# Batch 1's q and k transposed by TensorE instead of the DMA crossbar, in a fused attention and FFN kernel

## Chip, cores, metric

One core of one Trainium2 chip. The metric is the device time of one execution in microseconds (us). The kernel before took 269.71 us, the median of three runs (269.7 to 271.35); its profiled run took 265.9 us, with a span of 264.1 us in the trace.

## The reference

Block-sparse attention over 4 batches, 8 heads, 768 positions of 64 elements, then a multiplicative feed-forward layer:

```python
scores = (1/sqrt(64)) * q @ k.T           # per batch and head, 768 x 768
scores = where(mask, scores, -1e9)        # window, global and sampled 32-blocks
attn   = softmax(scores)
x      = (attn @ v), heads concatenated   # 3072 x 512
h      = (x @ w1) * (x @ w2)              # 512 -> 1024
out    = (h @ w3) @ w_out                 # the kernel folds w3 @ w_out into wf
```

## The kernel before

A planner in the program lists the work as tasks with guessed costs, orders them by a list schedule, and emits the instructions in that order. On the chip each engine then works through its own list in that order. In one unit of attention (a head pair and 256 queries) ScalarE takes the exponentials of scores (`e<-s`), VectorE multiplies by the mask and, after the value matmuls (`o<-v,e`), normalizes into `xn`.

q and k arrive with positions on the partitions and must be turned so that the 64 elements lie there. Batch 0 is turned by TensorE (`if b == 0`), the other batches by a relayout copy on VectorE and a transposing DMA from the SP queue:

```python
mid = ("qs", b, pr, x)                               # pool "qs" has 3 buffers
m = add(f"re {b}{pr}{x}", {DVE: 0.37}, ... nc.vector.tensor_copy(T(*mid), ...), deps=[LD[src]], ...)
t = add(f"xb {b}{pr}{x}", {SP: 1.25}, ... nc.sync.dma_start(out=T(*dst)..., in_=T(*mid)..., transpose=True),
        deps=[m], writes=[dst], reads=[mid], kind="xbar", prio=1)
```

The normalized rows `xn` go through the same crossbar, from the same SP queue, into `x`, which the w1 and w2 matmuls read. The planner's guess for a crossbar transfer hardly depends on what else the DMA engines do:

```python
elif t.kind == "xbar":
    xbar = max(xbar, t.end + 0.6) + t.bytes / 250e3
    t.seen = max(xbar + 0.4, t.end + (4.0 if lane > t.end else 1.2))
```

There is one accumulator buffer `o` in PSUM (where the matmuls write), two for the scores, and eight for the exponentials.

The softmax here doesn't subtract the row's maximum and nothing guards it: scores larger than these inputs give would overflow.

## Time and profile before

| | before, profiled run |
|---|---|
| span | 264.1 us |
| TensorE busy | 243.5 us (92%) |
| ScalarE, VectorE busy | 189.5, 174.8 us |
| mean granted clock (share of TensorE's full clock) | 0.948 |
| first w1 matmul | 71.04 us |

Loads move 14.7 MB as written, in 0.98 us for 192 KB, and fill the DMA engines up to about 85 us.

The prediction shows the slices, the waits and the hole at 45 to 52 us. A share of busy time says little here: the last 190 us are TensorE's without a gap, so only the first third has anything to win.

### The profile page before, as it was taken

The page shows a single profiled execution, that of the slowest core. Times are in us where ns is not written, and L with a number is a line of the kernel's source. Part 1 is how long each engine was busy: PE and PEld are TensorE (multiplying, and loading weights), DVE is VectorE, ACT ScalarE, POOL GpSimd, SP SyncE. Part 2 cuts the span into 40 slices and gives each one's busy share as a digit, 9 for nine tenths or more (in the row PEclk, how much of TensorE's full clock was granted, in tenths as well). Part 3 has the DMA queues.
Part 4 walks back from the last instruction along what each step waited for, and adds up shares of the span by engine and source line. Part 5 has one row for each costly group of instructions (what it writes and reads, how often), then busy time and mean ns, then how long its engine had stood idle before and what let it go on. Part 6 is the DMA issues. An engine that isn't in the chain of part 4 may idle for free.

```text
span 264.1 us, 6276 instructions
## 1 busy us (share of the span) xinstructions
PE 243.5 (92%) x2516; PEld 129.5 (49%) x2556; DVE 174.8 (66%) x381; ACT 189.5 (72%) x237; POOL 45.9 (17%) x75
## 2 busy tenths in 40 slices
PE   6888998099899999999999999999999999999993
PEld 2446655055454555554555455455554555444441
DVE  5585761268978888888888877857777787322420
ACT  3677766149988898998988988898987885324331
POOL 8943564512223112411000000000000000000000
PEclk9655799869999999999999999999999999999999
DMA  5999999999999819999229702033020231112013
GB/s 71 164 204 210 206 200 195 204 187 145 183 165 105 125 30 126 265 180 181 41 65 198 121 4 40 2 99 102 4 40 2 60 102 43 39 57 103 2 40 119
DMA packets 52193, 29.25 MB, mean 111 GB/s; under 512 B 33732, under 2 KB 47044, under 8 KB 52164
## 3 DMA queue, kind: packets, MB, share of 16 engines
q0 software_dynamic: 16416, 14.68, 37.1%
q1 hardware_dynamic: 35748, 14.16, 26.7%
q8 instruction: 20, 0.33, 0.5%
q14 instruction: 9, 0.07, 0.1%
HBM read 29.36 MB, written 6.29 MB: 135 GB/s over the span
## 4 chain that ended last, share of the span: by engine, by line
PE 84%; DMA 7%; ACT 3%; issue 3%; POOL 1%; DVE 0%; POOLq 0%; DVEq 0%; ACTq 0%
PE f L577 32%; PE f L596 16%; PE s L484 15%; PE o L506 15%; DMA qkt<-qs 5%; PE f L558 3%; ACT e L491 2%; DMA qn<-in_q_dram 2%; PE f L435 2%; PE f L412 2%; PE f L546 1%; ACT wf L271 0%; POOL qn L305 0%; DVE qs L444 0%; POOL kn L305 0%
## 5 line engine op out<-in xcount | busy, mean ns | idle before, releaser
L491 ACT ACTIVATE e<-s 128x1024 bf16<-128x1024 f32 x144 | 139.9, 1026 | 23.9 <-PE s L484 22.7
L493 DVE TENSOR_TENSOR e<-e,mask 128x1024 bf16<-128x1024 bf16 x144 | 94.0, 684 | 6.3 <-ACT e L491 6.1
L577 PE MATMUL f<-x,w 128*128 128x512 bf16 x361 | 93.2, 379 | 2.4 <-issue 1.3
L506 PEld LDWEIGHTS <-e 128*128 128x128 bf16 x1152 | 49.2, 100 | 36.7 <-DVE v L458 7.6
L506 PE MATMUL o<-v,e 128*128 128x65 bf16 x1152 | 57.8, 198 | 6.9 <-DVE v L458 6.8
L588 DVE TENSOR_TENSOR h<-f,a 128x512 bf16<-128x512 f32 x48 | 33.0, 687 | 28.7 <-PE f L577 26.9
L484 PE MATMUL s<-qkt 64*128 64x256 bf16 x576 | 47.8, 283 | 2.1 <-ACT e L491 1.6
L596 PE MATMUL f<-wf,h 128*128 128x512 bf16 x180 | 46.2, 379 | 0.8 <-issue 0.3
L577 PEld LDWEIGHTS <-w 128*128 128x128 bf16 x384 | 31.3, 97 | 29.4 <-issue 4.6
L585 ACT CAST a<-f 128x512 bf16<-128x512 f32 x48 | 28.2, 588 | 23.4 <-PE f L577 23.3
L484 PEld LDWEIGHTS <-qkt 64*128 64x128 bf16 x576 | 22.6, 95 | 30.9 <-issue 26.8
L596 PEld LDWEIGHTS <-h 128*128 128x128 bf16 x192 | 16.0, 98 | 14.7 <-issue 1.3
L514 DVE RECIPROCAL rec<-o 128x4 f32<-128x4 f32 x48 | 8.7, 180 | 20.0 <-PE o L506 19.8
L271 ACT COPY ob<-f 128x512 f32<-128x512 f32 x21 | 12.3, 587 | 13.1 <-PE f L596 11.9
L516 DVE TENSOR_TENSOR xn<-o,rec 128x256 bf16<-128x256 f32 x48 | 20.4, 424 | 1.7
L305 POOL DMA_DIRECT2D qn<-in_q_dram x16 | 11.6, 725 | 33.2 <-DVE qs L444 22.9
L305 POOL DMA_DIRECT2D vn<-in_v_dram x16 | 11.6, 723 | 27.9 <-DVE xn L516 19.0
L558 PE MATMUL f<-wo,w3t 128*128 128x512 bf16 x59 | 15.4, 392 | 0.8 <-ACT w3t L271 0.2
L305 POOL DMA_DIRECT2D kn<-in_k_dram x16 | 11.5, 721 | 20.8 <-DVE qs L444 13.9
L444 DVE COPY qs<-kn 128x768 bf16<-128x768 bf16 x12 | 4.3, 360 | 8.9 <-DMA qkt<-qs 8.9
L558 PEld LDWEIGHTS <-w3t 128*128 128x128 bf16 x64 | 5.8, 100 | 7.2 <-issue 1.5
L271 ACT CAST wf<-f 128x512 bf16<-128x512 f32 x8 | 4.7, 587 | 4.3 <-PE f L558 4.2
(50 smaller groups left out, 81.5 us busy)
## 6 DMA issues: line engine op xcount, KB each, us to landing
out_dram<-ob SPq DMA_DIRECT2D x24, 256.0 KB, 2.1
qn<-in_q_dram POOLq DMA_DIRECT2D x16, 192.0 KB, 6.3
kn<-in_k_dram POOLq DMA_DIRECT2D x16, 192.0 KB, 6.1
vn<-in_v_dram POOLq DMA_DIRECT2D x16, 192.0 KB, 7.3
w3n<-in_moe_w_dram POOLq DMA_DIRECT2D x8, 256.0 KB, 12.5
w<-in_moe_w_dram POOLq DMA_DIRECT2D x8, 256.0 KB, 10.0
wo<-in_moe_w_out_dram POOLq DMA_DIRECT2D x2, 512.0 KB, 11.0
qkt<-qs SPq DMA_TRANSPOSE x24, 6.4
```

The costliest lines, as they stand in the source:

```text
L271: (nc.scalar.copy if t.eng == ACT else nc.vector.tensor_copy)(out, in_)
L305: t = add(name, {POOL: 0.73}, lambda t: nc.gpsimd.dma_start(out=out_of(), in_=src), deps=deps, writes=writes, kind="load", prio=seq[0])
L484: nc.tensor.matmul(s[:, h, k2 * QT:(k2 + 1) * QT], lhsT=z[64 * h:64 * h + 64, 1, kc * 128:(kc + 1) * 128], rhs=z[64 * h:64 * h + 64, 0, t3 ...
L491: te = add(f"E {ek}", {ACT: 0.97}, lambda t, sk=sk, ek=ek: nc.scalar.activation(T(*ek), T(*sk), AF.Exp, scale=1.0 / 8.0), deps=[ts], reads ...
L493: tm = add(f"K {ek}", {DVE: 0.70}, lambda t, ek=ek, t3=t3, kp=kp: nc.vector.tensor_tensor(T(*ek), T(*ek), mask[:, t3, kp:kp + 1, :].to_bro ...
L506: nc.tensor.matmul(o[:, qt, h, :], lhsT=e[:, h, lo:lo + 128], rhs=w[:, h, kc, :], start=kc == 0 and qt == 0 and h == 0, stop=kc == C - 1, ...
L516: tx = add(f"xn {rk}", {DVE: 0.42}, lambda t, rk=rk, ok=ok, xk=xk, pr=pr: nc.vector.tensor_tensor(T(*xk)[:, :, 128 * pr:128 * pr + 128].re ...
L558: nc.tensor.matmul(T(*key), lhsT=T("w3t", i)[:, j, :], rhs=wo_sb[:, j, :], start=j == 0, stop=j == NF - 1)
L577: nc.tensor.matmul(T(*key), lhsT=w[:, c, f * 128:(f + 1) * 128], rhs=T(*xk)[:, c, :], start=c == 0, stop=c == 3)
L585: ta = add(f"a {i}{f}", {ACT: 0.58}, lambda t, ak=ak, key=ends["w1"][0]: nc.scalar.copy(T(*ak), T(*key)), deps=[ends["w1"][1]], reads=[end ...
L588: nc.vector.tensor_tensor(T(*hk)[:, f, :], T(*key), T(*ak), op=ALU.mult),
L596: nc.tensor.matmul(T(*key), lhsT=T(*hk)[:, f, n * 128:(n + 1) * 128], rhs=wf_sb[:, f, :], start=f == 0, stop=f == NF - 1)
```

## The change

Its intent: keep batch 1 off the crossbar while the loads run, and bring w1 and w2 in earlier so that the feed-forward matmuls can fill TensorE. The core of the diff:

```diff
-         "p10 p11 p12 p13 10 20 11 21 12 22 13 23 "        # loads: pairs of batch 1, then w1/w2
+         "10 20 11 21 12 22 13 23 p10 p11 p12 p13 "
-WARM = 8                                                  # warming matmuls at the start
+PRM = dict(..., trb=8, units="tttt", warm=0.0)            # one; "spare" ones never run at warm=0
-                xbar = max(xbar, t.end + 0.6) + t.bytes / 250e3
-                t.seen = max(xbar + 0.4, t.end + (4.0 if lane > t.end else 1.2))
+                at = t.start
+                for a, z, row in lanes:                   # every load in flight delays it
+                    if a < at + 1.25 <= z:
+                        at += 4.5 * row / 4096            # row: 4096 weights, 1536 q, k, v
+                t.end = at + 1.25
+                t.seen = t.end + 1.6 + 0.6 * (at - t.start)
-        "qs": ([128, C, 2, D], BF16, 3, None),
+        "qs": ([128, C, 2, D], BF16, 4, None),
-            if b == 0:
+            if (b, pr) in by_pe:                           # b * NP + pr < 8: batches 0 and 1
-                        prio=1)
+                        prio=1 if b == 0 else 4)
 ... (priority of the copies of batch 1; code for other unit orders, not used)
```

More of the change, by code (lines that the diff above doesn't have):

```diff
@@ L20 @@
 LOADS = ("a01 v00 a02 v01 a03 v02 v03 o0 o1 30 31 32 33 34 35 36 37 "
-         "p10 p11 p12 p13 10 20 11 21 12 22 13 23 "
+         "10 20 11 21 12 22 13 23 p10 p11 p12 p13 "
          "p20 p21 p22 p23 p30 p31 p32 p33")
-WARM = 8
 PRM = dict(bias=0.4, bmask0=1.0, bmask=1.0, btc=0.5, near=0.12, soon=0.06, kprio=2.0, eprio=0.5, aprio=1.0,
-           hprio=1.0, vprio=1.5, w3prio=10.0, ebufs=8, both=0.25, fo="31", pcopy=4.0)
+           hprio=1.0, vprio=1.5, w3prio=10.0, ebufs=8, both=0.25, fo="31", pcopy=4.0, trb=8, units="tttt",
+           warm=0.0)
 LONG = ("load", "xbar", "store")
@@ L51, in __init__ @@
         self.slots = defaultdict(list)
-        self.pool_of = {}
+        self.spare = None
     def add(self, name, costs, go, deps=(), writes=(), reads=(), kind="", prio=0, mode="N", flight=0.0, bias=None):
@@ L103, in run @@
         lane = 0.0
-        xbar = 0.0
+        lanes = []
         mode = "N"
@@ L132, in run @@
                     picks.append((p[0], eng, p[1]))
+            if self.spare and free["PE"] < PRM["warm"]:
+                pe = min([p[0] for p in picks if p[1] == "PE"], default=1e9)
+                rest = min([p[0] for p in picks if p[1] != "PE"], default=1e9)
+                if pe > free["PE"] + 0.2 and rest > free["PE"]:
+                    w = self.spare(mode)
+                    w.start, w.end, w.eng = free["PE"], free["PE"] + w.costs["PE"], "PE"
+                    free["PE"] = w.end
+                    self.log.append(w)
+                    continue
+            elif self.spare:
+                self.spare = None
+                self.left[("f", "warm")] = 0
+                self.freed[("f", "warm")] = free["PE"] + SEEN["PE"]
             picks.sort(key=lambda p: (p[0], p[1]))
@@ L141, in run @@
             if t.kind == "load":
-                lane = max(lane, t.end + 1.75) + t.bytes / 375e3
+                from_ = max(lane, t.end + 1.75)
+                lane = from_ + t.bytes / 375e3
+                lanes.append((from_, lane, t.row))
                 t.seen = lane + 0.2
@@ L146, in run @@
             elif t.kind == "xbar":
-                xbar = max(xbar, t.end + 0.6) + t.bytes / 250e3
-                t.seen = max(xbar + 0.4, t.end + (4.0 if lane > t.end else 1.2))
+                at = t.start
[3 more added lines that the diff above has]
+                t.end = at + 1.25
+                free[eng] = t.end
+                t.seen = t.end + 1.6 + 0.6 * (at - t.start)
                 for key in set(t.writes) | set(t.reads):
@@ L307, in load @@
         t.bytes = nbytes
+        t.row = 1536 if name.startswith("ld") else 4096
         return t
@@ L361, with spare @@
     t_zero = add("zero", {DVE: 0.2}, lambda t: nc.vector.memset(zero, 0.0), prio=-1)
-    for i in range(WARM):
-        add(f"warm {i}", {PE: 0.427}, lambda t: nc.tensor.matmul(
-            T("f", "warm"), lhsT=zero[:, :128], rhs=zero, start=True, stop=True),
-            deps=[t_zero], writes=[("f", "warm")], prio=-1)
+    add("warm", {PE: 0.43}, lambda t: nc.tensor.matmul(
+        T("f", "warm"), lhsT=zero[:, :128], rhs=zero, start=True, stop=True),
+        deps=[t_zero], writes=[("f", "warm")], prio=-1)
+    plan.users[("f", "warm")] += 1
+    def spare(mode):
+        rows = 64 if mode == "S" else 128
+        return Task("spare", {PE: 0.11}, (), (), (), lambda t: nc.tensor.matmul(
+            T("f", "warm")[:, :256], lhsT=zero[:rows, :128], rhs=zero[:rows, :256], start=True, stop=True),
+            "spare", 0, mode, 0.0)
+    plan.spare = spare
     def dve(name, cost, deps, go, **kw):
@@ L421 @@
     QK, V1 = {}, {}
+    by_pe = [(b, pr) for b in range(B) for pr in range(NP) if b * NP + pr < PRM["trb"]]
     def prepare(b, pr):
@@ L437, in prepare @@
                 m = add(f"tr {b}{pr}{x}", {PE: 0.35 + SWITCH}, tr, deps=[LD[src], t_ident], writes=[key], reads=[src],
-                        prio=1)
+                        prio=1 if b == 0 else 4)
                 done.append(add(f"tc {b}{pr}{x}", both(0.81, 0.56), lambda t, key=key, dst=dst, x=x: copy_on(
                     t, T(*dst)[:, x, :], T(*key, shape=[128, S], dt=BF16)), deps=[m], writes=[dst],
-                    reads=[key], prio=0, bias={ACT: -0.3 * x if pr == 0 else PRM["btc"]}))
+                    reads=[key], prio=0 if b == 0 else 3, bias={ACT: -0.3 * x if b + pr == 0 else PRM["btc"]}))
             else:
@@ L469 @@
     for b in range(B):
-        units += [(b, t, pr) for t in range(NT) for pr in range(NP)]
+        how = PRM["units"][b]
+        if how == "t":
+            units += [(b, t, pr) for t in range(NT) for pr in range(NP)]
+        elif how == "Q":
+            units += [(b, t, 2 * Q + i) for Q in range(2) for t in range(NT) for i in range(2)]
+        else:
+            units += [(b, t, pr) for pr in range(NP) for t in range(NT)]
     Xdone = defaultdict(list)
```

## The prediction

> **What bounds the kernel now.** I read the page's slices first, then the waits, then the timelines of the engines around the hole that the slices show, then the crossbar's own queue. Section 2 of the page, each column 6.6 us:
>
> ```profile
> PE   6888998099899999999999999999999999999993
> DVE  5585761268978888888888877857777787322420
> ACT  3677766149988898998988988898987885324331
> PEclk9655799869999999999999999999999999999999
> DMA  5999999999999819999229702033020231112013
> ```
>
> From the eleventh slice on TensorE is at 9 everywhere: the last 190 us are bound by matmul work, 98 to 99% busy (118.02 us busy of the 120 from 100 to 220 us, by a table of windows), with 3.9 us of ending after the last matmul. So time can only be won or lost in the first 75 us. There stands one hole, the eighth slice, where TensorE, VectorE and nearly ScalarE are all at 0 or 1 while the DMA engines stay at 9; right after it the granted clock is down too. The waits say who was held:
>
> ```profile
> DVE qs L444 <- DMA qkt<-qs: 9.3, 2, 8.9
> PE o L506 <- DVE v L458: 6.8, 1, 6.8
> ```
>
> and the timelines of VectorE, TensorE and the SP queue show the chain:
>
> ```profile
> 42.27 0.07 DVE L458 MEMSET v<- 128x12 bf16 x1
> 51.44 0.36 DVE L444 COPY qs<-kn 128x768 bf16<-128x768 bf16 x1 [8.88 <-DMA qkt<-qs]
> 51.71 0.17 DVE L514 RECIPROCAL rec<-o 128x4 f32<-128x4 f32 x1
> ...
> 44.72 0.84 PE L546 MATMUL f<-ident,w3n 128*128 128x128 bf16 x12
> 52.41 1.50 PE L506 MATMUL o<-v,e 128*128 128x65 bf16 x24 [6.84 <-DVE v L458]
> ...
> 71.04 1.02 PE L577 MATMUL f<-x,w 128*128 128x512 bf16 x3 [0.54 <-issue]
> ...
> 37.78 17.65 SPq L447 DMA_TRANSPOSE qkt<-qs  x4
> ```
>
> The fourth relayout copy of batch 1 needs one of three qs buffers; the first is free only when its crossbar transpose lands, 13.54 us after issue in the chain of the end. VectorE runs in order, so the reciprocal and normalization behind that copy wait too. They hold the only o accumulator, so the next value matmuls cannot start, and TensorE stands still from 45.5 to 52.4 us. The crossbar is slow because the loads fill the DMA engines: four transposes took 17.65 us to issue there, against 1.21 us for a single one at 135.62 us, when the queue is idle.
>
> The clock is the second loss. Windows of half a microsecond show it granted 0.50 from 50.3 to 57.15 us; TensorE was busy 4.52 of the 4.74 us from 52.41 on, so half of that, about 2.2 us, is lost.
>
> **What the Trainium skill says.** "TensorE: Matmul & The Clock Gate", Part 1, puts the clock down to half after an idle window of about 3.4 us and up again after a busy one. The trace agrees: it fell once 4.8 us into the hole and rose 4.7 us after work resumed. It is less simple at the start: the 0.50 from 9.37 to 29.85 us lay over a TensorE about 95% busy. Part 4 of the same page gives 275 to 390 ns for one transpose on TensorE and asks for a copy from PSUM after it. The trace has 314 ns median for one, but twelve in flight took 0.53 us at a granted 1.00 (0.46 us to the next matmul) and 0.71 to 0.77 us at 0.50, so the figure is a latency and the pitch is what counts. "DMA: Bandwidth & Descriptors", Queues, rings and completion order, says that each DMA engine takes turns between its queues by packet; that fits a crossbar transfer that stretches while the load queue is full. "TensorEngine Tiling (Array Packing)", Key Properties, says that a change of tiling mode drains TensorE; the 0.46 us above contains such a drain if there is one, so I add none.
>
> **The change, part by part.**
>
> 1. Batch 1's q and k by TensorE. The eight relayout copies on VectorE (8 x 0.36 = 2.9 us) and eight crossbar transposes go. The hole (6.84 us) goes with its cause, and the cold 6.8 us after it: 2.2 us. Added are 96 transposes: 8 groups x 0.46 = 3.7 us on TensorE, all on the bound, and eight copies from PSUM, four on ScalarE (0.80 each) and four on VectorE (0.56). If nothing else came into it: -6.84 - 2.2 + 3.7 = -5.3 us.
>
> 2. Loads behind w1 and w2. Load pitch in the trace is 0.98 us for a q, k or v and, by the bytes, 1.31 us for a weight block; 8 weight blocks move ahead of 9 smaller loads. From the issues I place the end of the w3 loads at about 34 us; then in the new order come 8 x 1.31 + 0.98 (one v of batch 0) = 11.5 us, so q of batch 1, pair 0 lands near 46.6 us, and each pair 2.9 us after the last. In the built order its transposes stand 9.5 us of work after the value matmuls of 44 us, at about 52 us; the second pair lands near 50 and is asked for near 56. I expect no wait for these loads.
>
> 3. What TensorE has to fill the time. This is the part that the diff hides, and the order shows. In the kernel before, the first w1/w2 matmul stands after 132 score matmuls (33 exponentials) and 240 value matmuls; in the changed one after 172 (43 exponentials) and 312. The wo/w3 products, which filled the gaps between 53 and 68 us before, are pulled forward into the place of the hole. After them there is a run of attention alone: 13 exponentials with nothing else for TensorE but two groups of transposes. There ScalarE sets the pace: two exponentials take 1.94 us, while their scores (8 in 0.54 us) and values (16 in 0.59) take 1.13.
>
>  Counting ScalarE: through 47.1 us both orders are the same, 19 exponentials. The score pair that follows the two value groups comes at about 48 us (V at 45.0, since six more wo/w3 products at 0.216 precede it; 0.9 + 0.43 + 0.55 + 0.9 + 0.27 of work after). From there to the first w1 matmul ScalarE does 22 exponentials x 0.97 = 21.3, four copies of 0.80 = 3.2 and one of 0.6: 25.1 us, to about 73.3 us. VectorE has about as much: from 45.9 us 26 mask products x 0.66, 11 normalizations x 0.56 and about 6 us of copies, 29 us, to the first product h near 75. TensorE's own work in that stretch is 240 V x 0.037 + 96 S x 0.0675 + 3.7 + 18 x 0.216 + 16 x 0.07 = 24 us, so it would be idle for some 4 to 5 us, in small pieces.
>
>  So the changed kernel starts w1 at 73.3 to 74.3 us rather than 71.04, but has done 40 score and 72 value matmuls more: 2.7 + 2.7 = 5.4 us of bound work. The lead is 5.4 - 2.3 to 3.3 = 2.1 to 3.1 us. After that both are bound by the same matmuls.
>
> 4. One warming matmul for eight. At the start the eight ran at 634 ns each and the clock stood at full for one window, 5.96 to 9.37 us by the clock records. With one, that window will likely be cold: twelve k transposes go from 0.53 to 0.85 us, and the first scores are late by as much. Cost about 0.3 us. The spare matmuls in the diff never run, as their limit is 0.
>
> 5. A fourth qs buffer and fewer crossbar transposes (24 to 16 for q and k) keep batches 2 and 3 from the same jam; there is no wait of that kind in TensorE's time after 75 us, so I give it nothing.
>
> Sum: -2.6 (middle of the lead) + 0.3 = -2.3 us by the trace. The trace's run took 265.9 us, though, and the timed ones 269.7; I do not know where those 3.8 us lie. If part of them is a longer hole or cold stretch, the change wins it back as well. I add a fifth of it, 0.8 us: 269.7 - 3.1 = 266.6.
>
> **The rivals.** (a) The hole closes and nothing takes its place: TensorE stays bound from 45 us on, which gives the -5.3 + 0.3 of step 1, 264.7 us; with the missing 3.8 us in the hole, 261. For it: two s and eight e buffers give slack, and x may come early. Against it: the engine's order is fixed, and the first w1 matmul stands behind the 43rd score group whatever x does. (b) ScalarE and VectorE become the bound for 15 us, as in step 3: 267.4, or 266.6 with the allowance. (c) The thin stretch of attention cools the clock: TensorE near 57% busy there, while it cooled at 9.37 us after a window 53% busy, but not at 46.9 after one of 60%. Two cold windows would cost 2 to 3 us: about 269. (d) A transpose stands in TensorE's order before its load has landed, and everything behind waits: each microsecond of lateness costs one. The 4 to 6 us of slack in step 2 speak against it. (e) The x transposes, now issued while weights stream, land late and hold the first w1 matmul: at 9.3 us to landing, seen before, the second pair, issued near 58, lands by 68, before 73.
>
> **Range and chances.** b is my main case with half the weight, a has a quarter, c, d and e share the rest. That gives 262.8 to 270.0 us for 8 in 10. The 2% line lies at 264.3 us; only a, or b with most of the unexplained 3.8 us, crosses it: 0.28. Slower than 275.1 would need c and d together: 0.03.
>
> **What would show it.** Step 1: no wait of VectorE for qkt<-qs, no zero in TensorE's slices, a clock at 9 from 30 us on, and about 3.7 us in 96 more transposes. Step 2: no wait of TensorE's transposes on qn or kn beyond the first pairs of batch 0. Step 3: first w1 matmul at 73 to 74 us, ScalarE over 90% busy from 55 to 72 us, TensorE idle 4 to 5 us from 46 to 74 in pieces under a microsecond. Step 4: a cold start up to about 30 us. I am wrong if w1 starts before 70 us (then a), if the clock falls between 60 and 75 us (c), or if TensorE has a wait over 2 us for a load or for x (d, e).

## More of the kernel before

From section 6 of the page, with the size in KB and the median microseconds from issue to landing as the last columns (a transpose has no size there):

```profile
w<-in_moe_w_dram POOLq DMA_DIRECT2D x8, 256.0 KB, 10.0
qkt<-qs SPq DMA_TRANSPOSE x24, 6.4
x<-xn SPq DMA_TRANSPOSE x24, 3.8
```

## The result, and the profile after

The changed kernel took 262.54 us, the median of 4 runs (261.72 to 264.28), against 270.53 us (269.7 to 273.14) for the kernel before: faster, ratio 0.970, 95% interval 0.961 to 0.978. Ratios here are the mean time of one kernel's fast runs over that of the other's in the same rounds, so not quite the ratio of the medians quoted. That it would be faster by over 2% was given a chance of 0.28, and the time lies just under the range (262.8 to 270.0).

The slices of the changed kernel, each 6.5 us:

```profile
PE   2988999999899999999999999999999999999993
DVE  5485942998988898889888877788787743412420
ACT  3577964999999688998898998888998844233321
PEclk9999999999999999999999999999999999999999
DMA  5999999999569699998427330212302033022013
```

The zero in TensorE's row is gone. The one soft place after the start is the eleventh slice (65 to 71 us), where ScalarE is at 9 and TensorE at 8. The clock's row needs care: the first clock record of this trace comes at 26.8 us, and the row shows 9 before it only because there is none. Twelve transposes took 0.85 us there, as they did at a granted 0.50, and 0.53 from 50 us on: the start was cold, as step 4 foretold.

The timeline of TensorE in the changed kernel (start, duration, line and operation, count):

```profile
44.03 0.89 PE L541 MATMUL o<-v,e 128*128 128x65 bf16 x24
...
46.50 0.61 PE L519 MATMUL s<-qkt 64*128 64x256 bf16 x8
...
50.09 0.53 PE L464 MATMUL f<-ident,qn 128*64 128x128 bf16 x12
...
71.95 0.39 PE L612 MATMUL f<-x,w 128*128 128x512 bf16 x1
```

Batch 1's first transposes run at 50.09 us and wait for nothing. The first w1 matmul comes at 71.95 us, 0.9 us later than in the profile of before, with 40 score and 72 value matmuls more behind it. By windows (busy time and count of TensorE, its weight loads, VectorE, ScalarE, GpSimd; then clock, DMA share, GB/s), the changed kernel:

```profile
44.00:60.00 16.00, 15.46 (x290) 10.87 (x293) 13.75 (x31) 14.70 (x18) 5.71 (x8) 1.00 1.44 166
60.00:75.00 15.00, 13.02 (x213) 8.08 (x213) 13.64 (x33) 14.60 (x17) 3.13 (x5) 1.00 0.74 107
75.00:100.00 25.00, 24.44 (x272) 12.81 (x275) 21.77 (x50) 20.71 (x26) 6.88 (x10) 1.00 0.99 123
```

and the kernel before in its recorded profile:

```profile
44.00:60.00 16.00, 8.94 (x122) 6.10 (x121) 5.95 (x16) 6.40 (x9) 4.97 (x7) 0.79 1.21 191
60.00:75.00 15.00, 13.54 (x191) 8.08 (x190) 12.63 (x32) 13.88 (x16) 4.29 (x6) 1.00 1.26 168
```

Read together: 6.5 us of TensorE's time come back between 44 and 60 us, and 0.5 us is given away between 60 and 75, where ScalarE is 97% busy (14.60 of 15). That is the mechanism of step 3. But spans of 264.1 and 259.5 us make 4.6 us, and the runs differ by 8.0. Where the rest lies was the first question for the chip.

### The profile page after: what moved, and what is told of

Read it like the earlier page. It is cut to its first block, busy times and chain, and to the rows that moved or that the text cites. A ratio compares the mean times of both kernels' runs of the same rounds, so it can differ in the third digit from the quotient of the medians.

```text
span 259.5 us, 6421 instructions
## 1 busy us (share of the span) xinstructions
PE 243.1 (94%) x2605; PEld 131.6 (51%) x2645; DVE 177.0 (68%) x380; ACT 190.3 (73%) x238; POOL 45.9 (18%) x75
## 4 chain that ended last, share of the span: by engine, by line
PE 86%; ACT 7%; issue 3%; DMA 2%; DVE 1%; POOL 0%; ACTq 0%; POOLq 0%
PE f L612 31%; PE f L631 16%; PE s L519 14%; PE o L541 14%; ACT e L526 6%; PE f L593 5%; PE f L464 3%; PE f L440 2%; DMA kn<-in_k_dram 2%; PE f L581 1%; ACT qkt L291 0%; DVE e L528 0%; DVE xn L551 0%; POOL qn L325 0%; ACT wf L291 0%
## 5 line engine op out<-in xcount | busy, mean ns | idle before, releaser
L612 PE MATMUL f<-x,w 128*128 128x512 bf16 x364 | 92.1, 379 | 1.5 <-issue 1.0
L541 PEld LDWEIGHTS <-e 128*128 128x128 bf16 x1152 | 47.7, 99 | 29.0 <-DVE xn L551 5.1
L541 PE MATMUL o<-v,e 128*128 128x65 bf16 x1152 | 56.4, 196 | 0.7 <-DVE e L528 0.2
L519 PE MATMUL s<-qkt 64*128 64x256 bf16 x576 | 48.4, 282 | 3.0 <-ACT e L526 2.5
L612 PEld LDWEIGHTS <-w 128*128 128x128 bf16 x384 | 32.0, 98 | 31.4 <-issue 4.2
L291 ACT COPY ob<-f 128x512 f32<-128x512 f32 x20 | 11.7, 587 | 15.1 <-PE f L631 14.0
L593 PE MATMUL f<-wo,w3t 128*128 128x512 bf16 x57 | 14.6, 379 | 0.6 <-ACT w3t L291 0.2
L464 PE MATMUL f<-ident,qn 128*64 128x128 bf16 x96 | 5.5, 268 | 3.8 <-DMA qn<-in_q_dram 3.0
L291 DVE COPY qkt<-f 128x768 bf16<-128x768 bf16 x10 | 5.6, 555 | 4.5 <-PE f L464 4.3
```

What stands on the lines that cost most here:

```text
L291: (nc.scalar.copy if t.eng == ACT else nc.vector.tensor_copy)(out, in_)
L519: nc.tensor.matmul(s[:, h, k2 * QT:(k2 + 1) * QT], lhsT=z[64 * h:64 * h + 64, 1, kc * 128:(kc + 1) * 128], rhs=z[64 * h:64 * h + 64, 0, t3 ...
L541: nc.tensor.matmul(o[:, qt, h, :], lhsT=e[:, h, lo:lo + 128], rhs=w[:, h, kc, :], start=kc == 0 and qt == 0 and h == 0, stop=kc == C - 1, ...
L593: nc.tensor.matmul(T(*key), lhsT=T("w3t", i)[:, j, :], rhs=wo_sb[:, j, :], start=j == 0, stop=j == NF - 1)
L612: nc.tensor.matmul(T(*key), lhsT=w[:, c, f * 128:(f + 1) * 128], rhs=T(*xk)[:, c, :], start=c == 0, stop=c == 3)
```

## The experiments

Sixteen kernels in four calls; each call had its own runs of the kernel before. All gave correct results. The median of before moved between 270.0 and 272.7 us from call to call, so medians are to be compared within a call. Before also scatters: 265.2 to 276.4 us over 44 runs, against 261.6 to 264.3 for the changed kernel. Because a run over 1.5% above its kernel's fastest is counted as slow and left out, the ratio depends on how lucky before's fastest run was. In the second call it was 265.23, and the changed kernel's ratio 0.983; in the fourth 270.98, and 0.961. By their 95% intervals, at a line of 2%, only v_x25 and the four kernels of the fourth call are faster than before, b_qs8 is slower, b_same is the same, and every other is unclear, all of the second call among them, where 9 of before's 11 runs count as slow. What the text compares are medians over all runs of a call.

One thing holds for every part below but the warming: an edit also moves the planner's order (the first w1 matmul stands after 33 to 48 exponentials), so that a part is always tested together with the order that it brings.

| call | run | what | median us (runs) | ratio |
|---|---|---|---|---|
| 1 | b_same | before again | 270.92 (6) | 1.008 |
| 1 | b_warm1 | before, one warming matmul | 270.04 (6) | 0.994 |
| 1 | a_warm8 | changed, eight warming matmuls | 261.74 (6) | 0.976 |
| 1 | a_qs3 | changed, three relayout buffers | 263.36 (6) | 0.982 |
| 2 | a_same | changed again | 262.38 (6) | 0.983 |
| 2 | b_pe | before, batch 1 by TensorE | 266.57 (6) | 0.999 |
| 2 | a_oldloads | changed, old order of loads | 265.91 (6) | 0.996 |
| 2 | a_trb4 | changed, batch 1 by crossbar | 270.98 (6) | 1.016 |
| 3 | b_pe_qs4 | b_pe with four buffers | 266.55 (6) | 0.978 |
| 3 | b_qs8 | before, eight buffers | 285.95 (6) | 1.052 |
| 3 | b_loads | before, new order of loads | 277.90 (6) | 1.018 |
| 3 | v_x25 | changed, milder crossbar guess | 263.82 (6) | 0.969 |
| 4 | a_ref | changed again | 261.79 (4) | 0.961 |
| 4 | a_oldxbar | changed, old crossbar guess | 259.27 (5) | 0.951 |
| 4 | v_ho60 | old loads, new guess from 60 us | 262.10 (6) | 0.962 |
| 4 | v_x35 | changed, guess between | 261.50 (4) | 0.960 |

### The kernel before again: where are the missing microseconds?

No edit.

> The kernel before again, unchanged, to see what its ordinary runs look like. Theory H (the jam of the crossbar is longer in most runs than in the one profiled run of 265.9 us): the mean granted clock and the span of its runs vary together, most runs at 268 to 273 us with a longer hole or a longer cold stretch than 50.3 to 57.15 us; its new profile shows the hole over 7 us. Theory W (fixed cost outside the span): the span is 264 in every run and only the time around it is longer.

Its new profile, of a run of 270.66 us, has a span of 268.9 us, and two holes rather than one. The slices of TensorE and its clock:

```profile
PE   6979994598089999999999999999999999999994
PEclk9655999599779999999999999999999999999999
```

The hole of the prediction sits in slices seven and eight; a second one is in the eleventh, with a second cold stretch that begins in it. The timeline of TensorE and that of the SP queue in this run:

```profile
50.18 1.50 PE L506 MATMUL o<-v,e 128*128 128x65 bf16 x24 [6.51 <-DVE v L458]
...
67.27 0.40 PE L484 MATMUL s<-qkt 64*128 64x256 bf16 x4 [0.26 <-ACT e L491]
74.44 0.59 PE L577 MATMUL f<-x,w 128*128 128x512 bf16 x1 [6.77 <-DMA x<-xn]
...
60.50 7.50 SPq L447 DMA_TRANSPOSE qkt<-qs  x2
68.10 3.61 SPq L529 DMA_TRANSPOSE x<-xn  x2
```

The first w1 matmul stands at the head of TensorE's list from 67.7 us on and waits for the second pair of x, which the SP queue could not issue before 68.1 us, since two crossbar transposes of batch 1 took 7.5 us there in front of it. The last `xn` of that pair was done at 61.23 us, so the pair stood 6.9 us in the queue. In the profile that the prediction read, the same pair was ready at 64.07 us, issued at 65.65 and landed at 70.95, 0.1 us before its use: by its time the one lucky run among the first four. The clocks of the 50 runs of before and b_same agree. Where a run's clock record leaves the cold start out (mean clock 0.973 and up), span times twice what is missing to 1 gives an estimate of how long it was cold later: 6.9 us in the run of 266.98 us, 10.7 in that of 268.67, and 13.4 to 14.6 in the seven from 270.31 to 272.74. One cold stretch is 6.8 us in both profiles, so this fits two in the usual run. Theory H holds, and W (a fixed cost outside the span) falls: span and run differ by 1.8 us in both profiles. The expected form was a longer first hole; it is a second one.

### The warming matmuls

```diff
-WARM = 8          # b_warm1: before with one      a_warm8: the changed kernel with eight
+WARM = 1
```

Every other instruction keeps its place in both.

> The kernel before with one warming matmul instead of eight; every other instruction keeps its place on every engine. Theory H: no gain, 0 to +0.5 us (the clock's early full window is lost), ratio 1.000 to 1.003. Rival R1 (the warming is what matters in the change): 2 to 4 us faster, ratio about 0.985.

> The changed kernel with eight warming matmuls again, all else in place. Theory H: as the changed kernel within 0.5 us, ratio to before 0.968 to 0.972. Rival R1: loses 2 to 4 us, ratio about 0.98 to 0.985.

270.04 us against 270.92 for before again, inside the scatter of both (265.6 to 272.1; 268.9 to 273.4), and 261.74 against 262.54 and 262.38 for the changed kernel. The warming is worth nothing that can be seen. b_warm1 alone would not exclude R1 (ratio 0.994, 0.985 to 1.002, unclear); a_warm8, whose six runs lie between 261.5 and 263.0, does, though its ratio of 0.976 misses the expected 0.968 to 0.972. R1 falls. In a_warm8 the first full clock came at 27.1 us although eight matmuls had run, so they did not even buy the early window every time.

### The fourth relayout buffer

```diff
-        "qs": ([128, C, 2, D], BF16, 4, None),
+        "qs": ([128, C, 2, D], BF16, 3, None),
```

> The changed kernel with three relayout buffers; the orders are the same for the first 40% of TensorE's list and differ after. Theory H: the fourth buffer gives nothing once batch 1 does not use the crossbar: ratio 0.967 to 0.974. Rival R2 (the fourth buffer carries part of the gain): 1 to 3 us slower than the changed kernel, ratio 0.975 to 0.98, with a wait of VectorE on the crossbar between 75 and 150 us.

263.36 us, with a span of 261.5 in the profile, which is of the slowest of the six runs. No wait of VectorE for the crossbar appears. The span's 2.0 us over the changed kernel's is there already at the first w1 matmul (73.85 against 71.95 us), before the orders part, and the clock explains it: it rose at 30.3 us instead of 26.8, and 3.6 us at half rate are 1.8 us of work. Its median stands 0.8 to 1.6 us above those of the changed kernel and a_warm8, which touches R2's range. But the spans of the six runs, 259.9 to 261.5 us with a mean of 260.6, are those of the changed kernel (259.5 to 261.2, mean 260.4, in ten runs): the excess lies outside the span, where run and span differ by up to 3.1 us here and, in nine of the ten, by about 2 there. Without a wait and without a longer span nothing is seen from the buffer in the changed kernel, and R2 falls for it.

### One part alone, one part undone

First the transposes alone on the kernel before, with the changed kernel beside it.

```diff
-            if b == 0:
+            if b <= 1:                    # and the change's priorities for batch 1
```

> The changed kernel again, unchanged, so that the part experiments of this call have it on the same chip. 261.5 to 264.5 us in every run, a spread of 3 us where the kernel before has 9; no wait of TensorE for a load or for x over 1 us after 30 us.

> The kernel before with batch 1 turned by TensorE alone: old order of loads, three relayout buffers, eight warming matmuls, old planner. Theory H2 (both holes of the kernel before come from batch 1's crossbar transposes on the SP queue, the first by the full relayout buffers, the second because the x transposes of batch 0 are queued behind them): both holes go, 261 to 265 us, at least three quarters of the 8 us gained. Rival R3 (the new order of loads is needed as well): a wait of TensorE over 2 us for w1 or w2 or x at the first w1 matmul, 265 to 269 us.

The transposes alone gave 266.57 us: 3.5 of the 7.6 us between the medians of this call. That is a miss; I had expected three quarters. The time lies in R3's range, but R3's wait at the first w1 matmul (65.89 us) is not there. The windows of b_pe show that the mechanism is right all the same, and where the rest goes:

```profile
44.00:60.00 16.00, 15.84 (x260) 9.75 (x260) 14.56 (x35) 14.58 (x18) 7.03 (x10) 1.00 1.23 188
60.00:75.00 15.00, 15.00 (x195) 8.38 (x192) 12.51 (x28) 14.05 (x17) 2.98 (x5) 1.00 1.05 142
75.00:100.00 25.00, 25.00 (x288) 13.17 (x285) 21.69 (x52) 21.42 (x27) 7.09 (x10) 1.00 0.83 116
100.00:120.00 20.00, 13.84 (x137) 6.62 (x135) 10.47 (x22) 10.71 (x15) 2.21 (x4) 0.91 1.41 164
```

Up to 75 us TensorE is fuller than in the changed kernel, and up to 100 it has no gap: both holes are gone, by the transposes alone. Then 6 us are lost between 100 and 120, where VectorE again waits for a crossbar transfer (5.6 us at the longest), this time of batch 2.

Then the order of loads, undone in the changed kernel:

```diff
-         "10 20 11 21 12 22 13 23 p10 p11 p12 p13 "
+         "p10 p11 p12 p13 10 20 11 21 12 22 13 23 "
```

> The changed kernel with the loads in the old order (batch 1 ahead of w1 and w2). Its order has the first w1 matmul after 192 score matmuls (48 exponentials) instead of 172. Theory H2: no hole over 2 us, but a longer stretch that ScalarE bounds: 2 to 4 us slower than the changed kernel, 264 to 266.5. Rival R3: over 267 us, with waits for loads.

265.91 us, as expected. The first w1 matmul comes at 76.09 us; between 60 and 75 us TensorE is busy 11.76 us and ScalarE 14.95. The clock fell at 76.2 us, after two windows in which TensorE was busy 2.24 and 1.64 of 3.41 us. It is rival (c) of the prediction, in another kernel.

And the transposes, undone in the changed kernel:

```diff
-PRM = dict(..., trb=8, ...)
+PRM = dict(..., trb=4, ...)
```

> The changed kernel with batch 1 turned by the crossbar again, behind w1 and w2, with four relayout buffers and the new planner. Theory H2: the crossbar is again what batch 1 and x wait for: a wait of TensorE or VectorE over 4 us for a crossbar transfer, 266 to 272 us. Rival R4 (the order of loads and the fourth buffer carry the gain): 260 to 263 us, since 3.7 us of transposes are saved.

270.98 us: nothing of the gain is left. R4 falls. The time was as expected, the wait not quite. On VectorE's timeline, and in the SP queue:

```profile
72.70 0.36 DVE L488 COPY v<-vn 128x768 bf16<-128x768 bf16 x1 [1.62 <-DMA vn<-in_v_dram]
78.78 0.37 DVE L488 COPY v<-vn 128x768 bf16<-128x768 bf16 x1 [2.69 <-DMA vn<-in_v_dram]
...
70.09 30.93 SPq L476 DMA_TRANSPOSE qkt<-qs  x12
```

Twelve crossbar transposes hold the SP queue for 31 us; no single wait for one is over 2 us, but they come late one after another, and VectorE meets v loads that have not landed in between.

### Buffers alone, loads alone, and the jam of batch 2

```diff
-        "qs": ([128, C, 2, D], BF16, 3, None),          # the kernel before
+        "qs": ([128, C, 2, D], BF16, 8, None),
```

> The kernel before with eight relayout buffers in place of three, nothing else. Theory H2: VectorE no longer waits in the first hole, but the crossbar transfers take as long as before and x stands behind them: a wait of TensorE for x or for qkt over 3 us remains, 266 to 271 us. Rival R2 (the buffers are the whole matter): 261 to 264 us and no hole over 2 us.

285.95 us, 13 us worse than before: outside both expectations. VectorE's first wait is gone, and the relayout copies run ahead. But that only fills the SP queue sooner. Four transposes take 20.5 us to issue (17.65 and 19.04 in the two profiles of before), and x, ready at 53.1 us, waits behind them until 64.7. TensorE's timeline, the SP queue's, and a row of the waits (total us, times, longest):

```profile
70.68 1.01 PE L577 MATMUL f<-x,w 128*128 128x512 bf16 x2 [10.18 <-DMA x<-xn]
125.51 1.03 PE L577 MATMUL f<-x,w 128*128 128x512 bf16 x2 [10.60 <-DMA x<-xn]
...
83.58 31.15 SPq L447 DMA_TRANSPOSE qkt<-qs  x10
...
PE f L577 <- DMA x<-xn: 20.8, 2, 10.6
```

The x that the first w1 matmul needs lands at 70.59 us, no later than in the kernel before (70.95, and 74.35 in b_same). TensorE, without its first hole, only reaches it sooner: up to there the hole has moved, and little is lost. The loss comes after. Ten more transposes hold the queue for 31 us, a later pair of x, ready at 105.5 us, is issued at 119.4, and TensorE waits a second time. So three buffers had also kept the copies from filling the queue that far ahead; as the order changes with them (VectorE's list parts from before's at 42 us), that this alone makes the 13 us is argued and not shown. Buffers do not help where the transfer itself is slow.

The new order of loads on the kernel before, the `LOADS` lines of the change and nothing else:

> The kernel before with w1 and w2 loaded ahead of batch 1, nothing else: batch 1 still by the crossbar with three buffers. Theory H2: no gain, 268 to 273 us, since the crossbar transfers of batch 1 now come later beside its own loads. Rival R3: 263 to 266.

277.90 us, 5 us worse than before and past the expected range: by the crossbar, batch 1 coming later is no gain; TensorE is busy only 12.46 of the 20 us from 100 to 120.

The buffer added to b_pe, to heal its jam at 104 to 116 us:

> The run with batch 1 turned by TensorE alone lost 6 us to a second jam at 104 to 116 us, now of batch 2: VectorE waits for a crossbar transfer with all three relayout buffers taken, then a cold clock. Here it has four buffers; the orders are the same up to about 85 us. Theory B (the buffers make that jam): 260 to 262.5 us, no wait of VectorE for qkt<-qs over 1 us. Rival D (the crossbar beside the late loads of batches 2 and 3 makes it, whatever the buffers): 265 to 267.5 us, scores or value matmuls wait between 100 and 120 us.

266.55 us. Theory B falls: the jam stands, four buffers or three. VectorE's and TensorE's timelines:

```profile
114.87 0.36 DVE L444 COPY qs<-kn 128x768 bf16<-128x768 bf16 x1 [6.94 <-DMA qkt<-qs]
...
116.48 0.62 PE L506 MATMUL o<-v,e 128*128 128x65 bf16 x8 [6.55 <-DVE e L493]
```

It is the first hole over again, 63 us later: a relayout copy waits for its buffer, and mask products behind it in VectorE's list wait too.

### The planner's model: a part that I had not counted

What was left between b_pe_qs4 (266.55, jam) and the changed kernel (none) was the order of loads and the planner's guess for a crossbar transfer. A first look at the guess was a try at a better kernel:

```diff
-                        at += 4.5 * row / 4096
+                        at += 2.5 * row / 4096        # v_x25; 3.5 in v_x35
```

> A try at a better one: the changed kernel with the planner's guess of a crossbar transfer's delay beside a weight load cut from 4.5 to 2.5 us, so that the first w1 matmul stands after 36 exponentials instead of 43. In the changed kernel x of the first unit landed near 63 to 65 us and was first used at 72, with TensorE idle 2 us between 60 and 75. Theory: 1 to 2.5 us faster than the changed kernel, 260 to 261.5 us. Rival: TensorE waits over 2 us for x at the first w1 matmul, 262 to 264 us.

263.82 us, no gain on the 261.8 to 262.5 of the changed kernel. It started w1 at 66.40 us as planned, but met a jam later: VectorE waited 2.82 us for the crossbar before 110.17 us, and TensorE then 2.25. That looked like proof that the new guess keeps batch 2 out of trouble, and I put that theory to the test by taking the guess alone out of the changed kernel:

```diff
-                at = t.start
-                for a, z, row in lanes:
-                    if a < at + 1.25 <= z:
-                        at += 4.5 * row / 4096
-                t.end = at + 1.25
-                free[eng] = t.end
-                t.seen = t.end + 1.6 + 0.6 * (at - t.start)
+                xbar = max(xbar, t.end + 0.6) + t.bytes / 250e3
+                t.seen = max(xbar + 0.4, t.end + (4.0 if lane > t.end else 1.2))
```

> The changed kernel once more, as the measure for the other three of this call: 261.5 to 264.5 us.

> The changed kernel with the planner's old model of a crossbar transfer (which hardly knows that loads slow it); transposes, loads and four buffers as in the changed kernel. Its first w1 matmul stands after 34 exponentials instead of 43. Theory P (the model is a part of the gain: it places batch 2's relayout copies where their buffers are free): a wait of VectorE for qkt<-qs of 2 us or more between 80 and 120 us, or of TensorE for x near 62 us, and 265 to 269 us. Rival L (the order of loads does it): 261 to 263.5 us, no wait over 1.5 us.

259.27 us (258.55 to 259.70), against 261.79 (261.56 to 261.96) for the changed kernel beside it: theory P falls, and rival L understated it. The old guess is 2.5 us better here. Its windows, and its first w1 matmul:

```profile
44.00:60.00 16.00, 15.74 (x296) 10.93 (x295) 13.21 (x28) 14.22 (x18) 6.15 (x9) 1.00 1.40 163
60.00:75.00 15.00, 14.18 (x189) 7.60 (x185) 12.34 (x30) 13.30 (x16) 3.84 (x6) 1.00 0.87 104
75.00:100.00 25.00, 25.00 (x284) 13.30 (x284) 21.76 (x50) 21.32 (x26) 5.72 (x8) 1.00 0.87 120
100.00:120.00 20.00, 20.00 (x249) 10.64 (x245) 17.09 (x39) 18.61 (x23) 4.28 (x6) 1.00 1.35 179
...
65.05 0.59 PE L608 MATMUL f<-x,w 128*128 128x512 bf16 x2 [0.55 <-DMA x<-xn]
```

The first w1 matmul stands after 34 exponentials instead of 43, and waits 0.55 us for x: the planner's optimism happened to be right to half a microsecond. Less attention runs with ScalarE as its bound, and no jam follows. The new guess, with weight loads at 4.5 us each, is too fearful in this place; that is why the thin stretch of the changed kernel is there at all.

The last but one goes back to the old order of loads, with one warming matmul and four buffers:

```diff
-         "10 20 11 21 12 22 13 23 p10 p11 p12 p13 "
+         "p10 p11 p12 p13 10 20 11 21 12 22 13 23 "
+                if t.start < 60:
+                    ... (the old guess)
+                else:
                     ... (the new guess)
```

> Old order of loads, batch 1 by TensorE, four buffers, one warming matmul; the planner keeps the old crossbar model up to 60 us of its plan and takes the new one from there. First w1 matmul after 37 exponentials, as in the run with TensorE's transposes alone, which had TensorE 100% busy from 60 to 100 us. Theory P: the jam at 104 to 116 us goes, 258 to 262 us, better than the changed kernel. Rival L: the jam stays, 265 to 267.5 us.

262.10 us. It keeps b_pe's full TensorE up to 100 us, and its wait of VectorE for a crossbar transfer is one of 2.8 us where b_pe_qs4's was 6.9 (TensorE then waits 2.36). So the new guess does help with the old order of loads, by 4.4 us over b_pe_qs4 in calls where the kernel before stood at 272.3 and 272.7. VectorE's list and those of the DMA queues are b_pe_qs4's up to about 100 us and ScalarE's throughout, so what helps is the order from there on. Used from the start, the new guess helps little: a_oldloads had 265.91. With the new order there is no such jam to heal.

> The changed kernel with the planner's guess cut from 4.5 to 3.5 us per weight load: first w1 matmul after 40 exponentials instead of 43. Theory P: about 1 us won at 60 to 75 us, and waits of VectorE for qkt<-qs between those of the changed kernel (none) and of the run with 2.5 (5.4 us): 261.5 to 263.5 us, within 1 us of the changed kernel. Rival (the idle time at 60 to 75 us is free to be had): 1 us or more faster.

261.50 against 261.79 us: 0.3 us, the w1 start at 70.71. Within the expectation of theory P, but with a_oldxbar known it says only that a guess in between buys little.

The version that beats both kernels is therefore the change without its new crossbar guess: 259.27 us against 261.79 and 272.33, ratio 0.951 to before (0.947 to 0.956).

## Why the prediction was right or wrong

Right, each by its own sign:

- The hole and its chain (the full relayout buffers, VectorE in order, the one accumulator, TensorE), and that turning batch 1 by TensorE removes it: no wait for qkt<-qs is left in VectorE's list of waits, no zero in the slices.
- The cold stretch behind the hole goes with it: the clock has one record from 26.8 us to 258.9.
- Step 2: transposes asked for at 50.09 us (foretold about 52), loads there before, no wait. Rival (d) did not come.
- The cost of a group of transposes: from the first group's start to the next matmul 0.46 us. A value group before one took 0.34 us to the next start where it takes 0.25 before a w1 matmul, so going over to a group of transposes costs about 0.1 us more, which I had left out: by estimate up to 0.8 us over eight groups.
- Step 3's mechanism: ScalarE was busy 16.70 of 17 us from 55 to 72 us, TensorE idled in pieces of under a microsecond.
- Step 4: a cold start, worth next to nothing.

Wrong: the size, by 4 us (266.6 foretold, 262.54 measured). Two terms of the sum were mis-sized and one part was not seen.

The step that failed is "I add a fifth of it, 0.8 us". The profile I read was the lucky run; the usual run of before has a second hole, which I could not see but might have inferred. Rival (e) had the right place with the wrong sign: I feared that x would land late in the changed kernel, where the SP queue is empty of batch 1, and did not ask how near to late it was in the kernel before, where the last x pair was issued at 65.65 us behind two qkt transposes and used at 71.04. The repeated profile of before has 268.9 us, 4.8 over the first, with a wait of 6.77 us that the first did not have: its first w1 matmul comes 3.4 us later, and the 2.69 us of work up to the end of the second cold stretch run at half clock, by estimate 1.3 us more. The term should have been nearly all of the 3.8 us.

The second is the lead in step 3, "2.1 to 3.1 us". Between the two profiles it was 5.4 - 0.9 = 4.5 us, which is the difference of the spans (4.6) almost exactly: after the first w1 matmul nothing more is won or lost. I had w1 at 73.3 to 74.3 us, it came at 71.95. Of that, 1.0 us is the value group that I put at 45.0 and that came at 44.03; the score pair behind it came 1.5 us before my 48. TensorE's idle time from 46 to 74 us was 2.5 us (25.53 busy of 28), not 4 to 5. A likely cause of that 1.0 us, argued and not shown, is the clock, which rose 3.0 us sooner in this run (26.8 against 29.7), worth up to half of that, 1.5 us; across all profiles that rise falls anywhere from 26.2 to 30.3 us, so this much is chance.

Three readings of the prediction are slightly off, without weight in its sum. Its clock records stand 0.13 us late (29.72, not 29.85, on the profile's own scale); cut at their right edges, the windows of rival (c) were 49 and 64% busy, not 53 and 60; and TensorE was 92% busy (18.74 of 20.48 us) in the cold start, not 95.

The part not seen is the planner's crossbar model. I listed five steps and took the model only as a mover of instructions; it costs 2.5 us in this kernel, and removing it is the best thing found. And the order of loads, which I had treated as a risk to survive (step 2), is a part of the gain: b_pe and a_oldloads each stop at about 266 us. With batch 1 on TensorE and four buffers, the new order of loads takes 266.55 (b_pe_qs4, third call) to 259.27 us (a_oldxbar, fourth) under the old guess, and 265.91 (a_oldloads) to 262.38 (a_same) under the new: it is worth 7.3 or 3.5 us there, and costs 5 us where batch 1 uses the crossbar. Taken alone on the kernel before, the parts gave 3.5 us (transposes), nothing (warming) or a loss (5 us for the loads, 13 for eight buffers); the gain of 8 us is no sum of them. The new guess alone, and four buffers alone, were not run on the kernel before.

What stays open: why the order of loads frees batch 2's crossbar transfers at 104 to 116 us. In b_pe_qs4 and in a_oldxbar nine q, k and v loads are issued between 92 and 118 us, and seven or eight qkt transposes; they differ in order and spacing. The nine loads are issued within 10.5 us in b_pe_qs4 (93.3 to 103.9) and within 21.0 us in a_oldxbar (95.3 to 116.3), which points at loads bunched beside the transposes; no run changes that alone. Nor was the x queue freed and nothing else changed. b_loads and a_trb4 come near: batch 1 stays on the crossbar, the second pair of x lands at 64.38 and 63.54 us, and yet both are no faster than before, because batch 1's own transposes then come late. So x in time is needed and is not enough.

## What to carry to other kernels

When one in-order queue carries two kinds of transfer, look at the one that is not late: how many microseconds it has to spare in this profile decides whether the next run has a hole there. More buffers in front of a slow transfer only move the wait, and can lengthen it. A profile is one run: where its time lies under the median of the others, profile the kernel again before sizing anything, and test a planner's cost model as a part of a change like any other.

## What the Trainium skill lacked or had wrong

- "DMA: Bandwidth & Descriptors", DMA Transpose (X-bar) and Queues, rings and completion order: neither says how far a transposing DMA slows beside a full load queue. Here a 128 x 768 one took 1.21 us to issue on quiet engines and 4.4 to 5.1 us each beside the loads (17.65 and 20.50 us for four), with a median of 12.1 us to landing from 30 to 85 us of b_qs8.
- The same page, Rules for kernel authors, lets a transpose stand "next to ordinary DMAs" with no more said; that holds for correctness, but two holes of 6.5 and 6.8 us in the kernel before (b_same) came of it.
- "TensorE: Matmul & The Clock Gate", Part 1: the clock is said to rise after one busy window of about 3.4 us. In the kernel before it stayed at half for 20.5 us under a TensorE 92% busy, also after the window from 22.9 to 26.3 us, 93% busy and without a transpose, and in every profile it rose for good, or until the first hole, only between 26.2 and 30.3 us. It fell without an idle window in a_oldloads, after two windows with TensorE 66 and 48% busy, and held in the changed kernel at 77% and more.
- The same page, Why this matters for your kernels, advises a warm-up of 4 us of matmuls for measuring; it does not say that a warm-up is lost if thinner work follows: in the kernel before, eight warming matmuls of 3.6 us bought full clock from 5.8 to 9.2 us only, and in a_warm8 none before 27.1 us, with no gain that could be seen (261.74 us, a_same 262.38 in another call).
- The same page, Part 4: 275 to 390 ns for a transpose is a latency. Twelve 128 x 64 transposes in a row cost 0.46 us at full clock, 38 ns each.
- "TensorEngine Tiling (Array Packing)", Key Properties: a change of mode drains TensorE, with no figure. Here a value group took 0.34 us to the next start before transposes and 0.25 us before w1 products; that the 0.1 us between them is such a drain is not shown.
